# Two PSUM banks as one tile, or as two tiles and later one: an attention and gated feed-forward kernel

## The chip, the cores and the metric

The kernel runs on one core of one Trainium2 chip. The metric is device time in microseconds (us); lower is better. Three runs of the kernel before gave 505.23, 505.27 and 505.43 us, median 505.27.

The engines are called as in the profile: PE (TensorE, with its weight loads as PEld), DVE (VectorE), ACT (ScalarE), POOL (GpSimd), SP (SyncE, which here only issues DMAs). PSUM is the memory that PE writes its products to, in eight banks; DVE and ACT read it.

## What is computed

Attention in chunks of 64 positions, then a feed-forward block with a gate made by a convolution over the sequence. Sizes: batch 8, 8 heads, sequence 576, head size 64, so x is 8 x 576 x 512; w_in is 512 x 1024, w_out 1024 x 512.

```python
scores = scale * q_c @ k_c.T                    # per chunk of 64 positions
attn = softmax(scores);  out = attn @ v_c
x = out.transpose(0, 2, 1, 3).reshape(B, S, H * D)
h = relu(x @ w_in)
conv_out[t] = w[0] * h[t - 1] + w[1] * h[t] + w[2] * h[t + 1]
y = (h * sigmoid(conv_out)) @ w_out
```

## The kernel before

The 4608 rows of x are worked in 36 tiles of 128 rows (two chunks each) for the attention, and in 16 units of 288 columns for the feed-forward. A unit has eight blocks, one for each 128 of the 1024 inner features. Each product with the weights is three matmuls on rounded high and low parts (`x_h`, `x_l`, `wi_h`, `wi_l` and so on).

A **block** is a chain over one PSUM bank: `mm1` (PE, L330, twelve matmuls of 128x290), `h_relu` (ACT, L337, in place in the bank), `c_mid` (ACT, L342, reads the bank), `c_left` and `c_right` (DVE, L346 and L352, read the bank), `c_sig` (ACT, L358, works on `c` in SBUF), `c_mul` (DVE, L361, reads the bank for the last time), then `g_hi` (ACT, L371) and `g_lo` (POOL, L375). An **output tile** is 24 matmuls `mm2` (PE, L384, 128x512) into one bank and one copy out `o_copy` (ACT, L389), which SP stores (L392). An **attention tile** is: transposes of q and k (`t_pe`, PE, L164, into a bank, copied out by ACT at L168; from tile 9 on DVE transposes from SBUF at L173), `scores` (PE, L196), the softmax, a transpose of the probabilities (`p_pe`, PE, L265, into a bank, copied out by ACT at L270, up to tile 11; later tiles use a DMA and DVE), `attn_v` (PE, L279), and the copies into `x_h` and `x_l` (ACT L315, DVE L319).

**The eight banks.** Two always belong to the scores (the tile `sx`, named `sx_ps`). Six, numbered 0 to 5 by the plan, rotate among `mm1`, `mm2`, the q and k transposes and the probability transposes; a step takes a bank (`take=[("bk", ...)]`) and another frees it. After attention tile 11 two of the six go to the scores for good: the steps `give_up` take them and hand out two more score slots (`sx_half`, slots 0 and 1). Which two these are comes out of the plan (`lent["y", 0]`, `lent["y", 1]`); here they are 0 and 2. In the kernel before they are the two halves of one tile of 2 x 512 columns, `pair` (named `y_ps`), from the first instruction to the last. So y_ps in the rows means: up to about 140 us bank 0 or bank 2 of the six, later the third and fourth bank of the scores. The other four are tiles of one bank each (`b1_ps`, `b3_ps`, `b4_ps`, `b5_ps`, shown as b_ps).

**What orders the work.** All steps are listed with costs and needs, and a long list of numbers (`order_`) sets their order by hand. Each engine runs its instructions in that order; nothing overtakes. The plan counts banks as six separate things. The waits between engines are not written by hand: the tile layer below the kernel puts a wait on every instruction that touches a tile for what touched the same tile before it on another engine.

Two plan steps, `lend` and `give_up`, stand on POOL at no cost and issue nothing. Ahead of the steps the last loop (L898 to L904) also puts in transposes of the identity (L902) where the plan sees PE idle in the first 110 us.

Of the kernel before, what the change touches and what calls it, by code (L numbers as in the profile page):

```python
# [20 lines left out]
F32 = mybir.dt.float32  # L21
# [5 lines left out]
PSUM = bass.MemoryType.PSUM  # L27
# [3 lines left out]
def attn_ffn(ctx: ExitStack, tc: tile.TileContext, q, k, v, w_in, conv_w, w_out, out):  # L31
# [4 lines left out]
    P = 128  # L36
# [32 lines left out]
    ps_b = ctx.enter_context(tc.tile_pool(name="ps_b", bufs=1, space=PSUM))  # L69
# [11 lines left out]
        return s  # L81

    sx = ps_s.tile([P, 2, 512], F32, name="sx_ps")
    pair = ps_b.tile([P, 2, 512], F32, name="y_ps")
    banks = [None] * 6
    ident = const.tile([P, P], F32, name="ident")
    make_identity(nc, ident)
    rebias = const.tile([P, 1], F32, name="rebias")
# [86 lines left out]
    def sx_half(i):  # L175

        cols = slice(G * C * (i % 2), G * C * (i % 2) + G * C)
        return (sx if i // 2 else pair)[:, :, cols]

    def sx_bank(i, u):  # L180
        return sx_half(i)[:, u, :]
# [2 lines left out]
        pass  # L184

    def give_up(st):
        pass

    def scores(st):

# [12 lines left out]
    def s_max(st):  # L203
        st["m"] = work.tile([P, 2, G], F32, name="m")
        sv = sx_half(st["s"]).rearrange("p u (g j) -> p u g j", j=C)
        nc.vector.tensor_reduce(out=st["m"], in_=sv, op=ALU.max, axis=AX.X)

    def s_sub(st):
        st["e"] = work3.tile([P, H, C], F32, name="e")
        nc.vector.tensor_tensor(  # L210
            out=st["e"].rearrange("p (g u) j -> p u g j", u=2), in0=sx_half(st["s"]).rearrange("p u (g j) -> p u g j", j=C),
            in1=st["m"].rearrange("p u (g o) -> p u g o", o=1).broadcast_to([P, 2, G, C]), op=ALU.subtract)
# [312 lines left out]
    def att(t, key, load_key, writes):  # L525
# [36 lines left out]
        if t == PAIR - 1:  # L562
            a = step("POOL", 0.0, key, give_up, (lent,), [s], take=[("bk", lent, ("y", 0))])
            step("POOL", 0.0, key, give_up, (lent,), [a], take=[("bk", lent, ("y", 1))], free=[("sx", "l0"), ("sx", "l1")])
# [53 lines left out]
    group_loads, before, lent = {}, {"new": [], "x": []}, {}  # L618
# [62 lines left out]
    for u in range(NU + 1):  # L681
# [15 lines left out]
        for i, t in enumerate(outs_in[u] if u <= NU - 1 else []):  # L697
            st = {}
# [153 lines left out]
    for i in order_:  # L852
# [4 lines left out]
        for r in s["take"]:  # L857
            r, st, name = (r, None, None) if isinstance(r, str) else (r + r[:1])[:3]
            since, b = min(free_buf[r])
# [26 lines left out]
        for r in s["free"]:  # L886
            r, name = (r, r) if isinstance(r, str) else r
            b = s["args"][0][name] if r in ("slot", "wslot", "sx", "bk") else held[r][0]
# [2 lines left out]
            if r == "bk":  # L891
                taken[b][-1][1] = end[i]

    lent_ = [lent["y", 0], lent["y", 1]]
    for i in range(6):
        banks[i] = pair[:, lent_.index(i), :] if i in lent_ else ps_b.tile([P, 512], F32, name=f"b{i}_ps")
    pe_free, until_ = 2.0, 110.0
    for i in sorted(order_, key=lambda i: begin[i]):  # L898
        if steps[i]["eng"] == "PE" and begin[i] <= until_:
# [37 lines left out]
```

## Time and profile before

One profiled execution, as the profile's page has it:

| | |
|---|---|
| time of the profiled execution | 505.31 us |
| its span, first to last instruction | 503.3 us, so 2.0 us lie around it |
| median of three runs | 505.27 us |
| PE busy | 488.8 us, 97% of the span |
| DVE, ACT, POOL busy | 353.2, 299.4, 194.4 us |
| granted TensorE clock | full, in all 40 slices |
| chain of work that ended last | 85% PE, 5% DVE, 4% SP |

The waits view says for each engine what it stood idle for; the timeline has in brackets the idle time ahead of an instruction and the instruction that ended it. Both leave out the shortest pauses. The windows view has the busy time of each engine in a stretch.

### The profile page before, as it was taken

The page shows a single profiled execution, that of the slowest core. Times are in us where ns is not written, and L with a number is a line of the kernel's source. Part 1 is how long each engine was busy: PE and PEld are TensorE (multiplying, and loading weights), DVE is VectorE, ACT ScalarE, POOL GpSimd, SP SyncE. Part 2 cuts the span into 40 slices and gives each one's busy share as a digit, 9 for nine tenths or more (in the row PEclk, how much of TensorE's full clock was granted, in tenths as well). Part 3 has the DMA queues.
Part 4 walks back from the last instruction along what each step waited for, and adds up shares of the span by engine and source line. Part 5 has one row for each costly group of instructions (what it writes and reads, how often), then busy time and mean ns, then how long its engine had stood idle before and what let it go on. Part 6 is the DMA issues. An engine that isn't in the chain of part 4 may idle for free.

```text
span 503.3 us, 12909 instructions
## 1 busy us (share of the span) xinstructions
PE 488.8 (97%) x4985; PEld 435.8 (87%) x4985; DVE 353.2 (70%) x736; ACT 299.4 (59%) x749; POOL 194.4 (39%) x261
## 2 busy tenths in 40 slices
PE   8899899989999999999999999999999999999997
PEld 8788779877779898999988989899988998999885
DVE  3889789585757597987866798889778785574300
ACT  4477887765445375675653767667556565685501
POOL 1352457522351334446170445433353606144300
PEclk9999999999999999999999999999999999999999
DMA  8989945433236565424657362335463021000102
GB/s 204 227 225 248 215 132 87 76 50 58 42 91 121 111 140 114 93 56 91 128 105 177 74 124 51 85 69 109 100 146 96 23 63 44 30 35 1 42 22 83
DMA packets 185905, 50.16 MB, mean 100 GB/s; under 512 B 175068, under 2 KB 178164, under 8 KB 185844
## 3 DMA queue, kind: packets, MB, share of 16 engines
q1 hardware_dynamic: 185844, 49.34, 43.8%
q8 instruction: 39, 0.64, 0.6%
q14 instruction: 22, 0.18, 0.1%
HBM read 36.72 MB, written 9.44 MB: 92 GB/s over the span
## 4 chain that ended last, share of the span: by engine, by line
PE 85%; DVE 5%; SPq 4%; ACT 3%; issue 1%; DMA 1%; POOL 0%; ACTq 0%; DVEq 0%; POOLq 0%
PE b_ps L384 38%; PE b_ps L330 34%; SPq L139 4%; PE y_ps L330 3%; PE sx_ps L196 2%; PE sx_ps L279 2%; PE y_ps L279 1%; PE b_ps L902 1%; PE y_ps L196 1%; DMA qk<-in_moe_w_in 1%; DVE wt L426 1%; DVE c L352 1%; PE b_ps L265 1%; DVE wt L431 1%; PE y_ps L384 1%
## 5 line engine op out<-in xcount | busy, mean ns | idle before, releaser
L375 POOL TENSOR_TENSOR g_l<-c,g_h 128x288 fp32r<-128x288 f32 (+8 forms) x184 | 111.1, 626 | 161.9 <-ACT g_h L371 154.3
L384 PE MATMUL b_ps<-wo_h,g_h 128*128 128x512 f32 x280 | 112.4, 402 | 0.6 <-DVE c L361 0.6
L384 PE MATMUL b_ps<-wo_h,g_l 128*128 128x512 f32 x280 | 110.4, 394 | 0.0
L384 PE MATMUL b_ps<-wo_l,g_h 128*128 128x512 f32 x280 | 110.3, 394 | 0.0
L346 DVE SCALAR_TENSOR_TENSOR c<-b_ps,cw,c 128x287 f32<-128x287 f32 (+1 forms) x116 | 59.0, 511 | 43.7 <-ACT c L342 43.6
L358 ACT ACTIVATE c<-c 128x288 f32<-128x288 f32 x128 | 56.3, 442 | 45.0 <-DVE c L352 44.4
L330 PE MATMUL b_ps<-x_h,wi_h 128*128 128x290 f32 x464 | 82.1, 299 | 0.4 <-ACT y_ps L337 0.4
L330 PE MATMUL b_ps<-x_l,wi_h 128*128 128x290 f32 x464 | 81.2, 297 | 0.0
L330 PE MATMUL b_ps<-x_h,wi_l 128*128 128x290 f32 x464 | 80.7, 296 | 0.0
L330 PEld LDWEIGHTS b_ps<-x_h,wi_h 128*128 128x128 f32 x464 | 72.0, 189 | 8.4 <-DVE c L361 1.1
L337 ACT ACTIVATE b_ps<-b_ps 128x290 f32<-128x290 f32 x116 | 46.1, 399 | 50.2 <-PE b_ps L330 49.7
L361 DVE SCALAR_TENSOR_TENSOR c<-c,b_ps 128x288 f32<-128x288 f32 x116 | 51.5, 446 | 27.1 <-ACT c L358 26.1
L330 PEld LDWEIGHTS b_ps<-x_l,wi_h 128*128 128x128 f32 x464 | 68.7, 190 | 0.3 <-DVE x_l L319 0.3
L330 PEld LDWEIGHTS b_ps<-x_h,wi_l 128*128 128x128 f32 x464 | 68.3, 189 | 0.0
L371 ACT CAST g_h<-c 128x288 fp32r<-128x288 f32 (+8 forms) x184 | 58.6, 357 | 10.8 <-DVE c L361 8.8
L384 PEld LDWEIGHTS b_ps<-wo_h,g_l 128*128 128x128 f32 x280 | 52.7, 188 | 12.3
L384 PEld LDWEIGHTS b_ps<-wo_h,g_h 128*128 128x128 f32 x280 | 52.8, 189 | 10.1 <-DVE c L361 1.2
L342 ACT ACTIVATE c<-b_ps,cw 128x288 f32<-128x288 f32 x116 | 57.4, 499 | 6.9 <-POOL g_l L375 0.4
L352 DVE SCALAR_TENSOR_TENSOR c<-b_ps,cw,c 128x288 f32<-128x288 f32 (+1 forms) x116 | 58.8, 511 | 2.6
L384 PEld LDWEIGHTS b_ps<-wo_l,g_h 128*128 128x128 f32 x280 | 52.7, 188 | 8.1
L241 POOL TENSOR_TENSOR wt<-wt,z 128x512 f32<-128x512 f32 x24 | 25.0, 1050 | 68.4 <-DMA qk<-in_k 21.7
L389 ACT ACTIVATE wt<-b_ps 128x512 f32<-128x512 f32 x35 | 20.8, 598 | 35.8 <-PE b_ps L384 33.7
(89 smaller groups left out, 589.8 us busy)
## 6 DMA issues: line engine op xcount, KB each, us to landing
out<-wt SPq DMA_DIRECT2D x36, 256.0 KB, 2.3
v<-in_v SPq DMA_DIRECT2D x21, 256.0 KB, 3.7
qk<-in_q SPq DMA_DIRECT2D x96, 48.0 KB, 2.3
qk<-in_k SPq DMA_DIRECT2D x96, 48.0 KB, 2.2
qk<-in_moe_w_out SPq DMA_DIRECT2D x4, 1024.0 KB, 5.9
v<-in_v SPq DMA_DIRECT2D x48, 64.0 KB, 4.2
wt<-wt SPq DMA_DIRECT2D x48, 64.0 KB, 2.1
qk<-in_q SPq DMA_DIRECT2D x96, 24.0 KB, 1.9
```

Of the source, the lines that this page charges most:

```text
L241: nc.gpsimd.tensor_tensor(out=two(st, "to"), in0=two(st, "of"), in1=z, op=ALU.mult)
L330: nc.tensor.matmul(h_ps[:, 0:hi - lo], lhsT=wt[:, f // 2, kt, P * (f % 2):P * (f % 2) + P], rhs=xt[:, u % NX, kt, 0:hi - lo], start=n == 0 ...
L337: nc.scalar.activation(out=h, in_=h, func=AF.Relu)
L342: nc.scalar.mul(out=st["c"], in_=banks[st["h"]][:, i0:i0 + st["n"]], mul=cw[:, FT + f:FT + f + 1])
L346: nc.vector.scalar_tensor_tensor(out=c[:, a:n], in0=banks[st["h"]][:, i0 + a - 1:i0 + n - 1], scalar=cw[:, f:f + 1], in1=c[:, a:n], op0=AL ...
L352: nc.vector.scalar_tensor_tensor(out=c[:, 0:b], in0=banks[st["h"]][:, i0 + 1:i0 + 1 + b], scalar=cw[:, 2 * FT + f:2 * FT + f + 1], in1=c[: ...
L358: nc.scalar.activation(out=st["c"], in_=st["c"], func=AF.Tanh, scale=0.5)
L361: nc.vector.scalar_tensor_tensor(out=st["c"], in0=st["c"], scalar=1.0, in1=banks[st["h"]][:, st["i0"]:st["i0"] + st["n"]], op0=ALU.add, op ...
L371: nc.scalar.copy(out=g_h[:, f, gs], in_=st["c"][:, cs])
L375: nc.gpsimd.tensor_tensor(out=g_l[:, f, gs], in0=st["c"][:, cs], in1=g_h[:, f, gs].bitcast(F32), op=ALU.subtract)
L384: nc.tensor.matmul(banks[st["o"]], lhsT=gt[:, f, o:o + P], rhs=wt[:, f, :], start=f == 0 and n == 0, stop=f == FT - 1 and n == 2)
L389: nc.scalar.mul(out=st["os"], in_=banks[st["o"]], mul=0.5)
```

## The change

The two lent banks are no longer one tile. They come as two tiles of one bank each from a pool of their own, `ps_y`. When `give_up` runs for the second time, while the program is being built, that pool is closed, and a new pool `ps_z` is opened in its place, with one tile `z_ps` of 2 x 512 columns that holds both banks. `sx_half` takes that tile for slots 0 and 1. No instruction is added, taken away or put elsewhere on any engine; the tiles lie in other banks (sx 0 and 1 as before; the four b tiles in 2 to 5 instead of 4 to 7; the lent pair in 6 and 7 instead of 2 and 3).

```diff
     sx = ps_s.tile([P, 2, 512], F32, name="sx_ps")
-    pair = ps_b.tile([P, 2, 512], F32, name="y_ps")
     banks = [None] * 6
+    ps_y = ExitStack()
...
-        return (sx if i // 2 else pair)[:, :, cols]
+        return (sx if i // 2 else lent["pair"])[:, :, cols]
...
     def give_up(st):
-        pass
+
+        st["given"] = st.get("given", 0) + 1
+        if st["given"] == 2:
+            ps_y.close()
+            st["pair"] = ctx.enter_context(tc.tile_pool(name="ps_z", bufs=1, space=PSUM)).tile([P, 2, 512], F32, name="z_ps")
...
-    lent_ = [lent["y", 0], lent["y", 1]]
+    early_banks = ps_y.enter_context(tc.tile_pool(name="ps_y", bufs=1, space=PSUM))
     for i in range(6):
-        banks[i] = pair[:, lent_.index(i), :] if i in lent_ else ps_b.tile([P, 512], F32, name=f"b{i}_ps")
+        banks[i] = (early_banks if i in (lent["y", 0], lent["y", 1]) else ps_b).tile([P, 512], F32, name=f"b{i}_ps")
```

What the diff does not show is which waits stand on the instructions. The next rows are ACT's, around the first probability transpose that uses a lent bank; y_ps_86 is the pair, and each wait names the engine it is for.

```order
L270 COPY pT_799<-y_ps_86 128x512 [waits DVE_49,PE_49]
L315 CAST x_h_99<-sx_ps_85 128x4x128
L219 ACTIVATE e_754<-e_754 128x512
L371 CAST g_h_101<-c_656 128x288 [waits DVE_49]
L337 ACTIVATE y_ps_86<-y_ps_86 128x290 [waits PE_49,Activation_49]
L467 CAST wo_h_97<-wt_712 128x1024 [waits DVE_49]
L168 COPY qT_835<-y_ps_86 128x512 [waits Activation_49]
```

The same seven instructions of the changed kernel; b0_ps_108 and b2_ps_110 are the two lent banks.

```order
L274 COPY pT_803<-b2_ps_110 128x512 [waits PE_49]
L319 CAST x_h_98<-sx_ps_85 128x4x128 [waits DVE_49,PE_49]
L223 ACTIVATE e_758<-e_758 128x512
L375 CAST g_h_100<-c_660 128x288 [waits DVE_49]
L341 ACTIVATE b0_ps_108<-b0_ps_108 128x290 [waits PE_49]
L471 CAST wo_h_96<-wt_716 128x1024 [waits DVE_49]
L168 COPY qT_839<-b2_ps_110 128x512 [waits PE_49]
```

The instructions and their order are the same (lines are four further down). The copy of the probabilities, pT, reads bank 2; it no longer waits for DVE, and its wait for PE is for its own four transposes instead of for the `mm1` that PE puts into bank 0 after them. `h_relu` on bank 0 waits for its own `mm1` instead of for the q transposes that PE puts into bank 2 after it.

On PE the same is seen a little earlier. These six rows of before are the `mm1` into bank 1, then the transposes of the probabilities into bank 2 (y_ps_86), then `attn_v`.

```order
L330 MATMUL b1_ps_106<-x_h_99,wi_h_95 128x290 x4
L330 MATMUL b1_ps_106<-x_l_100,wi_h_95 128x290 x4
L330 MATMUL b1_ps_106<-x_h_99,wi_l_96 128x290 x4
L265 MATMUL y_ps_86<-ident_87,e_634 128x128 [waits DVE_49,Activation_49,Pool_49]
L265 MATMUL y_ps_86<-ident_87,e_634 128x128 x3
L279 MATMUL sx_ps_85<-pT_652,v_602 64x64 [waits DMAHW2_49,DVE_49]
```

And of the changed kernel:

```order
L334 MATMUL b1_ps_109<-x_h_98,wi_h_94 128x290 x4
L334 MATMUL b1_ps_109<-x_l_99,wi_h_94 128x290 x4
L334 MATMUL b1_ps_109<-x_h_98,wi_l_95 128x290 x4
L269 MATMUL b2_ps_110<-ident_86,e_638 128x128 [waits Pool_49]
L269 MATMUL b2_ps_110<-ident_86,e_638 128x128 x3
L283 MATMUL sx_ps_85<-pT_656,v_606 64x64 [waits DMAHW2_49,DVE_49]
```

The first transpose keeps its wait for POOL, which makes its input, and has lost the two for DVE and ACT, which were for `c_right` and `c_mid` on bank 0. Over the whole program 63 of 6166 instructions on the five engines wait for something else than before, all of them up to the handing over of the two banks; the first matmul into `z_ps` waits for DVE, ACT and a DMA, as the first into the scores' half of the pair did.

## The prediction

> **What bounds the kernel now.** I read the page first, then the windows view in four stretches, then who waits for whom inside the one that has idle time, then the timeline around the pauses.
>
> ```profile
> span 503.3 us, 12909 instructions
> ...
> PE 488.8 (97%) x4985; PEld 435.8 (87%) x4985; DVE 353.2 (70%) x736; ACT 299.4 (59%) x749; POOL 194.4 (39%) x261
> ```
>
> ```profile
> 0.00:39.00 39.00, 35.28 (x488) 32.49 (x489) 26.39 (x52) 21.75 (x38) 13.38 (x16) 1.00 0.89 224
> 39.00:132.00 93.00, 85.96 (x888) 76.27 (x887) 72.75 (x146) 67.81 (x163) 41.79 (x45) 1.00 0.54 115
> 132.00:450.00 318.00, 317.99 (x3364) 285.05 (x3364) 241.44 (x514) 190.38 (x495) 125.99 (x175) 1.00 0.42 91
> 450.00:503.30 53.30, 49.61 (x250) 42.01 (x248) 12.66 (x26) 19.43 (x55) 13.27 (x26) 1.00 0.09 35
> ```
>
> The columns are the stretch, its length, busy time of PE, PEld, DVE, ACT and POOL, then clock and DMA. PE sets the time: 97% of the span, and from 132 to 450 us 317.99 of 318.00. So time gained on PE before 132 comes off the end one for one, if nothing else holds it up later. The first 39 us hold filler transposes and first loads, and the last 53 the tail; the change has nothing there to remove but a small part. What is to be had lies in 39 to 132: 93.00 - 85.96 = 7.04 us of idle PE. PE's waits there, in total us, times, longest:
>
> ```profile
> PE y_ps L330 <- DVE c L361: 1.4, 2, 0.7
> PE y_ps L330 <- ACT y_ps L337: 1.1, 1, 1.1
> PE y_ps L330 <- ACT c L342: 0.9, 1, 0.9
> PE y_ps L330 <- DVE c L352: 0.8, 1, 0.8
> PE y_ps L265 <- DVE c L361: 0.7, 1, 0.7
> PE y_ps L164 <- ACT pT L270: 0.7, 1, 0.7
> PE b_ps L384 <- DVE c L361: 0.6, 1, 0.6
> PE y_ps L384 <- ACT c L342: 0.4, 1, 0.4
> PE b_ps L330 <- ACT y_ps L337: 0.4, 1, 0.4
> ```
>
> Ten pauses, 7.0 us, and they account for all of the idle time. Eight stand before a matmul that writes y_ps, though y_ps is two of six banks. And the releasers are odd. A matmul may begin a bank anew when `c_mul` (L361) has read it for the last time; here PE goes on after `h_relu` (L337), `c_mid` (L342) or `c_right` (L352), with `c_mul` of that block still to come. So the bank that PE writes is not the bank that was being read: it is the other half of the pair.
>
> **What the pairing costs, seen at one place.** Timeline rows: start, length, what, and in brackets the idle time before it and who ended it. The first two show an undisturbed `mm1` for comparison.
>
> ```profile
> 40.02 0.69 PE L330 MATMUL y_ps<-x_h,wi_h 128*128 128x290 f32 x4
> 40.56 0.70 PE L330 MATMUL y_ps<-x_l,wi_h 128*128 128x290 f32 x4
> ...
> 49.82 0.59 ACT L270 COPY pT<-y_ps 128x512 f32<-128x512 f32 x1 [1.71 <-PE y_ps L330]
> 50.46 0.66 PE L164 MATMUL y_ps<-ident,qk 128*128 128x128 f32 x4 [0.68 <-ACT pT L270]
> ...
> 53.72 0.51 ACT L342 ACTIVATE c<-y_ps,cw 128x288 f32<-128x288 f32 x1
> 54.28 0.81 PE L330 MATMUL y_ps<-x_h,wi_h 128*128 128x290 f32 x4 [0.92 <-ACT c L342]
> 54.92 0.71 PE L330 MATMUL y_ps<-x_l,wi_h 128*128 128x290 f32 x4
> ```
>
> At 49.82 ACT copies transposed probabilities out of bank 2. What it copies is written by L265, yet it stood idle 1.71 us for an L330, the `mm1` into bank 0. Having been held, it holds PE at 50.46, whose transposes need bank 2. At 54.28 PE begins an `mm1` in bank 2 and has waited for `c_mid` on bank 0.
>
> Each stop costs more than its idle time. Undisturbed, four matmuls last 0.69 us but the next four begin 0.54 after them (40.02 to 40.56): 0.15 overlap, lost when PE drains. After the stop the step from the first four to the next is 0.64 (54.28 to 54.92), 0.10 more. So a stop costs its idle time and about 0.25 us.
>
> ACT and DVE pay too. Of their waits in the same stretch, those released by a matmul that makes nothing they read:
>
> ```profile
> ACT c L342 <- PE y_ps L330: 2.4, 2, 1.5
> ACT pT L270 <- PE y_ps L330: 1.7, 1, 1.7
> ACT pT L270 <- PE y_ps L384: 1.6, 1, 1.6
> DVE c L346 <- PE y_ps L330: 3.7, 2, 2.0
> DVE c L361 <- PE y_ps L330: 2.1, 1, 2.1
> DVE c L361 <- PE y_ps L384: 1.0, 1, 1.0
> ```
>
> 5.7 us on ACT and 6.8 on DVE. `c_mid` and `c_left` come after `h_relu` of their own bank, so by then their `mm1` is long done.
>
> **The change, part by part.** *Two tiles in place of one, up to the handing over.* It takes off waits, and adds and moves no instruction, DMA or queue. Five of the eight y_ps pauses lose the wait that ended them, since that reader is on the other bank: the two released by L342, those released by L352 and L337, and, by the waits of the built programs, one of the two L330 released by L361. The other three have a true last wait that came late: the copy at 49.82 for 50.46, and twice a `c_mul` that DVE reached late (for the other L330, and for L265). The two pauses before b_ps are of the same kind, one bank further off:
>
> ```profile
> 105.64 0.50 ACT L342 ACTIVATE c<-y_ps,cw 128x288 f32<-128x288 f32 x1 [0.95 <-PE y_ps L330]
> 105.87 0.50 PE L384 MATMUL b_ps<-wo_h,g_h 128*128 128x512 f32 x1 [0.64 <-DVE c L361]
> 107.19 0.76 PE L330 MATMUL b_ps<-x_h,wi_h 128*128 128x290 f32 x4 [0.37 <-ACT y_ps L337]
> ```
>
> At 105.64 `c_mid` waits 0.95 us for a foreign `mm1`, and ACT and DVE, each in its order, bring everything behind it late, the `c_mul` of banks 1 and 3 among it. So I take all ten: 7.0 us idle + 10 x 0.25 = 9.5 us.
>
> What is late next? DVE has 72.75 us of work for the stretch; in 93.0 - 9.5 = 83.5 us that is 87%, with 10.8 us of room, and 6.8 us of what it now idles goes away as well. ACT has 67.81, or 81%. Loads: none of these waits of PE names a DMA. I charge nothing for a new wait, and keep it as a rival.
>
> *The new pool and its tile.* The first scores in `z_ps` must wait for the last readers of both lent banks. The latest is a `c_mul`; PE, behind which everything would stand, comes there much later (a row of the timeline, and one of the chain of waits: start, length, what):
>
> ```profile
> 139.76 0.40 DVE L361 SCALAR_TENSOR_TENSOR c<-c,y_ps 128x288 f32<-128x288 f32 x1
> ```
>
> ```profile
> 150.87 0.62 PE y_ps L279 x32
> ```
>
> 150.87 - 140.16 = 10.7 us of room. PE and that `c_mul` move forward together, so it costs nothing; were PE's whole gain not shared by DVE, 1.2 us would still be left. Nor does the choice of bank numbers: no row ties a length to one.
>
> *After the handing over* PE needs its loads earlier by as much as it comes earlier. SP's queue, its waits in 130 to 172 us and its rows on either side of the longest:
>
> ```profile
> SPq L392 <- ACT wt L389: 10.4, 1, 10.4
> ```
>
> ```profile
> 130.66 2.58 SPq L156 DMA_DIRECT2D v<-in_v  x4
> 143.71 2.05 SPq L392 DMA_DIRECT2D out<-wt  x2
> ```
>
> SP stands 10.4 us at 143.71 behind the store of an output tile, which waits for `o_copy`, so for PE. With PE 9.5 us ahead, the store and the loads queued behind it come 9.5 us ahead, just inside SP's own 133.24. So the loads move along.
>
> **Sum.** The profiled execution took 505.31 us (span 503.3, 2.0 around it), as good as the median of 505.27. 505.3 - 9.5 = **495.8 us**. If the rest of this holds, 494.3 to 497.3: less 1.5 if three stops keep half their price; and 1.5 better, since the view leaves out short stops, and the twelve `mm1` blocks in the pair could each hide 0.12 us.
>
> **Rivals.** A difference of 0.2% (1.0 us) is about what a measurement of this kernel can tell from none.
>
> *Real shortage of banks.* The pauses would mean that six banks are too few, and new true waits would take the place of the old. For it: the two pauses before b_ps. Against: from 140 us on the same two products have four banks, and PE is never idle up to 450. If half of the stops stay, the gain is 4.7 us: 500.6. The Trainium skill (Perfetto Trace Analysis, Optimization Strategy) says that a gap that keeps repeating on the engine that should be saturated can mean too little PSUM for the next tile; read so, all ten stops would stay, and the time with them. The trace speaks for that only as far as the two b_ps rows go. Chance 0.13.
>
> *The gain is given back after 132 us.* SP has only 0.9 us between its own end (133.24) and the new time of that store (134.2). If issue or landing of the loads, and not PE, sets the pace from there, PE runs dry by up to 9.5 us before 175 and the kernel ends at 505.3. Against: SP's 10.4 us wait. Chance 0.04.
>
> *The change doesn't do what it says*, the layer below still tying the two tiles together: 505.3. The rows of waits speak against it. Chance 0.02.
>
> *Slower: DVE becomes the bound.* More of DVE's work would fall beside POOL's (41.79 us here), and if they slow each other, DVE's 72.75 us grow. PE comes out behind once DVE needs over 93 us, a stretch of 28%; at 35% it needs 98.2 and the time is about 510.5. Against: POOL is busy in 45% of this stretch already (41.79 of 93), and `c_right` on the pair has this spread (shortest, median, longest ns):
>
> ```profile
> L352 DVE SCALAR_TENSOR_TENSOR c<-y_ps,cw,c x12: 474/516/518, 45.7 to 138.3; 128x288 f32<-128x288 f32 x6, 128x287 f32<-128x287 f32 x6
> ```
>
> No instruction there is stretched. Chance 0.02.
>
> **How the numbers follow.** The forecast has 0.79, the shortage 0.13, the gain given back 0.04, no effect of the edit 0.02, slower 0.02. The range takes the forecast's bounds and reaches into the shortage, to where a little under half of the stops stay: 494.3 to 499.5. Faster 0.79 + 0.13 = 0.92, same 0.04 + 0.02 = 0.06, slower 0.02.
>
> **What would show it.** Right: idle PE in the stretch that now is 39 to 132 falls from 7.04 us to under 1, no PE wait between 39 and 123 us named for a reader of another bank, no ACT L270 released by an `mm1`, the first `attn_v` in the new tile at about 141.4 instead of 150.87, SP's longest wait before its store still there but short, and PE without idle from there to the tail. Wrong: PE pauses of the same number before the lent banks (shortage, or no effect), or PE idle between 130 and 175 behind SP or a DMA (given back), or DVE instructions longer than in the rows above (slower).

## The result and the profile after

The changed kernel took 497.84 us (median of 4 runs, 497.11 to 498.99), before 505.35 on the same chip: ratio 0.985, 95% interval 0.9827 to 0.9873. The forecast was 495.8 us, in a range of 494.3 to 499.5. The profiled execution took 497.11 us. In the code after, lines are four further down (`mm1` is L334, `attn_v` L283, `p_pe` L269, `c_mul` L365, `w_sgn` L435, POOL's subtraction `w_left` L439, ACT's cast `w_hi` L471).

The head of the page and its engines, after:

```profile
span 495.1 us, 12901 instructions
...
PE 484.8 (98%) x4985; PEld 435.6 (88%) x4985; DVE 353.1 (71%) x736; ACT 298.6 (60%) x749; POOL 194.5 (39%) x261
```

PE's busy time fell by 4.0 us with the same 4985 matmuls: a stop costs more than its idle time, and the rest counts as busy (of the 10.0 us that the ten places returned, see below, 7.0 were idle). The stretches, in the windows view (length, then PE, PEld, DVE, ACT, POOL, clock, DMA):

```profile
0.00:39.00 39.00, 32.45 (x472) 29.46 (x473) 26.47 (x49) 20.17 (x36) 12.31 (x16) 1.00 0.87 210
39.00:123.00 84.00, 84.00 (x898) 77.96 (x897) 73.42 (x150) 68.19 (x164) 41.84 (x44) 1.00 0.59 130
123.00:132.00 9.00, 9.00 (x73) 7.30 (x72) 6.18 (x14) 4.59 (x11) 1.05 (x3) 1.00 0.35 64
132.00:441.00 309.00, 309.00 (x3297) 278.24 (x3296) 233.65 (x499) 185.40 (x484) 125.91 (x174) 1.00 0.43 93
```

All ten pauses are gone: from 39 us to the tail PE is never idle. But the first stretch got worse: 32.45 us busy in 39 where before had 35.28. PE's longest wait of the whole program, after:

```profile
PE sx_ps L283 <- ACT wi_h L471: 2.2, 1, 2.2
...
```

This line is new; the view has four more, all in the first 39 us, and all of them were there before. (One of them, at 11.24 us, grew from 0.17 to 0.92 us, but only because PE came to it 0.75 us sooner.) Pairing every matmul with the same matmul of before gives the whole account, in the times of the changed kernel: it is 2.08 us late after 32.72 us, level with before at 54.4, 7.94 us ahead at 120, and 8.2 ahead from 300 us to the end. So the ten places, with shorter ones between them, returned 10.0 us, later places 0.3, and one new place took 2.1: 505.31 - 8.2 = 497.1.

The new place, in the timeline of before (start, length, engine, line):

```profile
26.96 0.59 ACT L168 COPY qT<-y_ps 128x512 f32<-128x512 f32 x1 [0.55 <-PE y_ps L265]
27.92 1.06 ACT L467 CAST wi_h<-wt 128x1024 fp32r<-128x1024 f32 x1
28.52 0.69 DVE L431 SCALAR_TENSOR_TENSOR wt<-qk,wt 128x512 uint32<-128x512 uint32 x1
29.06 3.63 POOL L435 TENSOR_TENSOR wi_l<-wt,wi_h 128x1024 fp32r<-128x1024 f32 x2 [1.58 <-ACT wi_h L467]
30.64 0.69 PE L279 MATMUL sx_ps<-pT,v 64*64 64x64 f32 x32
```

and after:

```profile
26.30 0.57 ACT L168 COPY qT<-b_ps 128x512 f32<-128x512 f32 x1
27.25 1.06 ACT L471 CAST wi_h<-wt 128x1024 fp32r<-128x1024 f32 x1
28.38 2.37 POOL L439 TENSOR_TENSOR wi_l<-wt,wi_h 128x1024 fp32r<-128x1024 f32 x1 [0.91 <-ACT wi_h L471]
28.51 2.78 DVE L435 SCALAR_TENSOR_TENSOR wt<-qk,wt 128x512 uint32<-128x512 uint32 x1
31.93 0.69 DVE L214 TENSOR_TENSOR e<-sx_ps,m 128x512 f32<-128x512 f32 x1
32.72 0.69 PE L283 MATMUL sx_ps<-pT,v 64*64 64x64 f32 x32 [2.24 <-ACT wi_h L471]
```

Read them from the top. ACT's copy of qT lost a false wait for the transposes of `p_pe` in the other lent bank, and starts 0.66 us sooner. Its cast wi_h does too, so POOL's subtraction starts at 28.38 instead of 29.06. DVE's `w_sgn` stands where it stood, at 28.5, but POOL is now 0.13 us ahead of it, and `w_sgn` takes 2.78 us instead of 0.69, until just after POOL's end at 30.75. The `attn_v` at 32.72 overwrites what DVE's L214 reads, so it waits for that (31.93 + 0.69 = 32.62); the view names ACT's wi_h, which had ended at 31.95.

### The profile page after: what moved, and what is told of

The parts are those of the page before. It is cut to its first block, busy times and chain, and to the rows that moved or that the text cites. A ratio compares the mean times of both kernels' runs of the same rounds, so it can differ in the third digit from the quotient of the medians.

```text
span 495.1 us, 12901 instructions
## 1 busy us (share of the span) xinstructions
PE 484.8 (98%) x4985; PEld 435.6 (88%) x4985; DVE 353.1 (71%) x736; ACT 298.6 (60%) x749; POOL 194.5 (39%) x261
## 4 chain that ended last, share of the span: by engine, by line
PE 93%; DVE 4%; DMA 1%; ACT 1%; issue 1%; ACTq 0%; DVEq 0%
PE b_ps L334 42%; PE b_ps L388 41%; PE sx_ps L283 3%; PE sx_ps L200 3%; PE z_ps L283 1%; DVE wt L435 1%; PE b_ps L164 1%; PE z_ps L200 1%; PE b_ps L906 1%; DMA qk<-in_moe_w_in 1%; PE b_ps L269 1%; DVE wt L430 1%; DVE wt L425 0%; DVE z L230 0%; DVE e L214 0%
## 5 line engine op out<-in xcount | busy, mean ns | idle before, releaser
L350 DVE SCALAR_TENSOR_TENSOR c<-b_ps,cw,c 128x287 f32<-128x287 f32 (+1 forms) x128 | 65.1, 510 | 46.0 <-ACT c L346 45.8
L334 PE MATMUL b_ps<-x_h,wi_h 128*128 128x290 f32 x512 | 90.7, 299 | 0.0
L334 PE MATMUL b_ps<-x_l,wi_h 128*128 128x290 f32 x512 | 89.5, 297 | 0.0
L334 PE MATMUL b_ps<-x_h,wi_l 128*128 128x290 f32 x512 | 89.1, 296 | 0.0
L334 PEld LDWEIGHTS b_ps<-x_h,wi_h 128*128 128x128 f32 x512 | 79.3, 189 | 7.8 <-DVE c L365 0.6
L365 DVE SCALAR_TENSOR_TENSOR c<-c,b_ps 128x288 f32<-128x288 f32 x128 | 56.6, 445 | 29.0 <-ACT c L362 28.0
L334 PEld LDWEIGHTS b_ps<-x_l,wi_h 128*128 128x128 f32 x512 | 75.9, 190 | 0.0
L334 PEld LDWEIGHTS b_ps<-x_h,wi_l 128*128 128x128 f32 x512 | 75.4, 189 | 0.0
L346 ACT ACTIVATE c<-b_ps,cw 128x288 f32<-128x288 f32 x128 | 63.2, 499 | 7.3 <-POOL g_l L379 0.4
L356 DVE SCALAR_TENSOR_TENSOR c<-b_ps,cw,c 128x288 f32<-128x288 f32 (+1 forms) x128 | 64.8, 510 | 2.8
L388 PEld LDWEIGHTS b_ps<-wo_h,g_h 128*128 128x128 f32 x288 | 54.4, 189 | 9.2
```

Source lines behind the costliest of these rows:

```text
L334: nc.tensor.matmul(h_ps[:, 0:hi - lo], lhsT=wt[:, f // 2, kt, P * (f % 2):P * (f % 2) + P], rhs=xt[:, u % NX, kt, 0:hi - lo], start=n == 0 ...
L346: nc.scalar.mul(out=st["c"], in_=banks[st["h"]][:, i0:i0 + st["n"]], mul=cw[:, FT + f:FT + f + 1])
L350: nc.vector.scalar_tensor_tensor(out=c[:, a:n], in0=banks[st["h"]][:, i0 + a - 1:i0 + n - 1], scalar=cw[:, f:f + 1], in1=c[:, a:n], op0=AL ...
L356: nc.vector.scalar_tensor_tensor(out=c[:, 0:b], in0=banks[st["h"]][:, i0 + 1:i0 + 1 + b], scalar=cw[:, 2 * FT + f:2 * FT + f + 1], in1=c[: ...
L365: nc.vector.scalar_tensor_tensor(out=st["c"], in0=st["c"], scalar=1.0, in1=banks[st["h"]][:, st["i0"]:st["i0"] + st["n"]], op0=ALU.add, op ...
L388: nc.tensor.matmul(banks[st["o"]], lhsT=gt[:, f, o:o + P], rhs=wt[:, f, :], start=f == 0 and n == 0, stop=f == FT - 1 and n == 2)
```

## The experiments

Three theories of what was seen. **Collision** (the texts written before the runs call it the port theory): `w_sgn` reads two tiles of SBUF, POOL's subtraction reads SBUF, and whichever starts first holds up the other; the loss is 2.1 us, and the order of the two is all that matters. **Load**: `w_sgn` was long because its data came late or by chance. **Banks**: part of the gain or loss comes from the new pool and the new bank numbers. All kernels but one are the changed kernel with a list of added waits: ("ACT", 19, "PE", 220) makes ACT's instruction number 19, counted from 0, wait for PE's number 220.

**The changed kernel once more**, on the chip of the next three, as a control.

> The changed kernel, unaltered, once more, as the ground for the other three. Two theories. Port theory: one DVE instruction at about 28.5 us (the last step of preparing a weight block, 0.69 us before, 2.78 us in the profile of the changed kernel) is held by a POOL instruction that starts 0.1 us ahead of it, because an ACT copy lost a wait and the chain from ACT to POOL came 0.67 us earlier; this is in the program, so it is there in every execution: again 2.7 to 2.8 us, time 497 to 499. Load theory: the 2.1 us slip between 28 and 36 us comes of when the loads landed in that execution; then the DVE instruction is 0.7 us in some executions, and the time of this run may be 495.5.

498.06 us (497.18 to 498.82), ratio 0.9845 [0.9824, 0.9867]. Its profiled execution took 498.48 us, with these waits of PE among others:

```profile
PE sx_ps L283 <- ACT wi_h L471: 2.4, 1, 2.4
...
PE b_ps L334 <- issue: 0.8, 1, 0.8
...
PE b_ps L164 <- DMA qk<-in_k: 0.4, 1, 0.4
```

The new wait is there again. The two small ones and 0.2 us on the first are the 1.4 us by which this span (496.5) is longer than the first one's. The long `w_sgn` in both executions speaks against the load theory.

**ACT's false wait back.** The qT copy alone waits again for the `p_pe` in the other bank.

```diff
+    waits = [("ACT", 19, "PE", 220)]
```

> The changed kernel with one of the lost waits put back: ACT's copy of the transposed q at about 26.3 us waits again for the probability transposes in the other lent bank. Nothing else differs. Port theory: the copy is back at 26.96 us, POOL's instruction back at about 29.06, behind the start of the DVE instruction, which takes 0.69 us again; 2.1 us come off the changed kernel, to about 495.7 us, although a wait was added. Load theory: the loads are as they were, the time is that of the changed kernel, 497 to 499.

494.88 us (494.68 to 495.21), ratio 0.9786 [0.9772, 0.9801]: 3.2 us under the changed kernel on the same chip, and no run of the one reaches a run of the other. The collision accounts for 2.1 of the 3.2 (the spans of the profiled executions are 495.1 and 492.9 us). The other 1 us is that the runs of the changed kernel spread from 497.1 to 499.0, and these only from 494.7 to 495.2; why, no run shows. Its timeline at the place:

```profile
26.98 0.58 ACT L168 COPY qT<-b_ps 128x512 f32<-128x512 f32 x1 [0.55 <-PE b_ps L269]
...
28.54 0.69 DVE L435 SCALAR_TENSOR_TENSOR wt<-qk,wt 128x512 uint32<-128x512 uint32 x1
...
29.08 3.63 POOL L439 TENSOR_TENSOR wi_l<-wt,wi_h 128x1024 fp32r<-128x1024 f32 x2 [1.58 <-ACT wi_h L471]
...
30.66 0.70 PE L283 MATMUL sx_ps<-pT,v 64*64 64x64 f32 x32
```

A wait that is good for nothing in itself makes the kernel faster: DVE is first again, `w_sgn` takes 0.69 us, and PE starts at 30.66 without a pause that the view shows.

**POOL waits instead.** All false waits stay away; POOL's subtraction waits for `w_sgn`.

```diff
+    waits = [("POOL", 9, "DVE", 35)]
```

> The changed kernel with one new wait: POOL's instruction at 28.4 us (low part of a weight block, 128x1024) waits until the DVE instruction that it held up is done. ACT's copy stays early. Port theory: POOL starts at about 29.3 instead of 28.4, DVE takes 0.69 us, and 2.1 us come off: 495.7 us, as with the wait put back by the other means. Load theory: no change, 497 to 499.

495.62 us (495.22 to 496.17), ratio 0.9801 [0.9786, 0.9816].

```profile
28.63 0.69 DVE L435 SCALAR_TENSOR_TENSOR wt<-qk,wt 128x512 uint32<-128x512 uint32 x1
...
29.47 3.60 POOL L439 TENSOR_TENSOR wi_l<-wt,wi_h 128x1024 fp32r<-128x1024 f32 x2 [1.88 <-ACT pT L274]
30.76 0.69 PE L283 MATMUL sx_ps<-pT,v 64*64 64x64 f32 x32 [0.16 <-issue]
```

ACT is early here and DVE is still not held, so it is POOL's start that decides, not ACT's. Both came out within 1 us of the 495.7 that the collision theory gave. The load theory falls.

**The pair one tile, the new pool kept.** The two lent banks are one tile until they are given up; pool, handing over and bank numbers are those of the changed kernel, and the waits on the instructions are those of before.

```diff
+    lent_ = [lent["y", 0], lent["y", 1]]
+    pair = early_banks.tile([P, 2, 512], F32, name="y_ps")
     for i in range(6):
-        banks[i] = (early_banks if i in (...) else ps_b).tile([P, 512], F32, name=f"b{i}_ps")
+        banks[i] = pair[:, lent_.index(i), :] if i in lent_ else ps_b.tile([P, 512], F32, name=f"b{i}_ps")
```

> One part undone: the two lent banks are one tile again until they are given up, but in a pool of its own that is closed then, with the new tile in its place as in the changed kernel, and at the changed kernel's bank numbers. Coupling theory (the single tile tied two unrelated banks together, and PE's ten pauses came of it): all of the gain is gone, 505.3 us, with PE's pauses of 7.0 us back. Rival (the new pool or the other bank numbers bring the gain): 497 to 499, or something between.

505.63 us (504.94 to 506.7), ratio 0.9999 [0.9989, 1.001]. Every pause of before is back at its place and length; three of the ten in its timeline of PE:

```profile
112.77 0.78 PE L334 MATMUL y_ps<-x_h,wi_h 128*128 128x290 f32 x4 [0.65 <-DVE c L365]
123.16 0.77 PE L334 MATMUL y_ps<-x_h,wi_h 128*128 128x290 f32 x4 [0.80 <-DVE c L356]
126.80 0.80 PE L334 MATMUL y_ps<-x_h,wi_h 128*128 128x290 f32 x4 [1.11 <-ACT y_ps L341]
```

So pool and bank numbers bring nothing; the tying of the two banks is the whole effect, of both signs.

**Whose waits were they?** The kernel with ACT's wait back (494.88) is the changed one without the collision, and before is that kernel with all other false waits. The next two put back one half each: PE's twelve, or the other 39, on ACT and DVE; with ACT's wait, these are all that the tied pair adds. They and the last two kernels ran on another chip, on which before took 505.3 us instead of 505.5; differences to 494.88 are good to a few tenths of a us.

```diff
+    waits = [("ACT", 19, "PE", 220), ("PE", 428, "DVE", 62), ("PE", 428, "ACT", 45), ...]
```

> The kernel with ACT's wait (494.88 us), and the twelve waits that PE's instructions had through the pairing put back as well; ACT's and DVE's stay away. Bounds: 494.88 us without any of them, 505.5 with all. Step of the prediction: five pauses, 3.9 us idle in all, were ended by a foreign reader on PE itself, and five more, 3.1 us, came from ACT and DVE being late. If both halves add up, with 0.25 us a stop, this kernel costs 3.9 + 5 x 0.25 = 5.1 us: 500.0. Rival 1, PE's own waits are the whole: 505. Rival 2, they bite only because ACT and DVE are late, and alone cost little: under 496.5.

496.45 us (496.29 to 496.48), ratio 0.9824 [0.981, 0.9837]: 1.6 us, not 5.1. All of PE's pauses between 39 and 132 us:

```profile
52.88 0.79 PE L334 MATMUL b_ps<-x_h,wi_h 128*128 128x290 f32 x4 [0.36 <-ACT c L346]
85.44 0.50 PE L388 MATMUL b_ps<-wo_h,g_h 128*128 128x512 f32 x1 [0.17 <-ACT c L346]
```

The counterpart:

```diff
+    waits = [("ACT", 19, "PE", 220), ("ACT", 43, "PE", 387), ("ACT", 44, "ACT", 43), ..., ("DVE", 60, "PE", 387), ...]
```

> The counterpart: the kernel with ACT's wait (494.88 us), and the other waits of ACT and DVE for work in the foreign bank put back; PE's stay away. If the halves add up: 3.1 us idle in five pauses, with 5 x 0.25 us, 4.4 us: 499.3. Rival 1 (PE's own waits are the whole): 495. Rival 2 (lateness of ACT and DVE is the whole): 505. If this kernel and its counterpart together cost clearly more or less than the 10.6 us between 494.88 and 505.5, the waits of the engines feed each other.

501.08 us (500.61 to 501.31), ratio 0.9915 [0.9901, 0.9928]: 6.2 us. Its pauses in the same stretch:

```profile
50.70 0.66 PE L164 MATMUL b_ps<-ident,qk 128*128 128x128 f32 x4 [0.68 <-ACT pT L274]
53.79 0.81 PE L334 MATMUL b_ps<-x_h,wi_h 128*128 128x290 f32 x4 [0.20 <-ACT qT L168]
59.97 0.80 PE L334 MATMUL b_ps<-x_h,wi_h 128*128 128x290 f32 x4 [0.72 <-DVE c L365]
69.38 0.63 PE L269 MATMUL b_ps<-ident,e 128*128 128x128 f32 x4 [0.72 <-DVE c L365]
104.65 0.50 PE L388 MATMUL b_ps<-wo_h,g_h 128*128 128x512 f32 x1 [0.64 <-DVE c L365]
105.97 0.78 PE L334 MATMUL b_ps<-x_h,wi_h 128*128 128x290 f32 x4 [0.36 <-ACT b_ps L341]
```

The halves cost 1.6 and 6.2 us, together 7.8 of the 10.6 us between this base and before; the other 2.8 us need both. With PE's waits alone PE hardly ever stops, since ACT and DVE are then early enough. Held themselves by a foreign matmul, they come late to the reads for which PE waits: the pauses at 112.77, 123.16 and 126.80 above stand in neither half.

**Can the collision of before be had too?** Before already has one at 20 us, in its timeline:

```profile
18.72 1.04 POOL L258 TENSOR_TENSOR e<-e,z 128x512 f32<-128x512 f32 x1 [7.15 <-DVE z L232]
19.05 1.79 DVE L426 SCALAR_TENSOR_TENSOR wt<-qk,wt 128x1024 uint32<-128x1024 uint32 x1
19.73 2.26 POOL L435 TENSOR_TENSOR wi_l<-wt,wi_h 128x512 fp32r<-128x512 f32 x1
20.88 2.18 DVE L431 SCALAR_TENSOR_TENSOR wt<-qk,wt 128x1024 uint32<-128x1024 uint32 x1
```

The two DVE instructions, with two SBUF inputs each, take 1.79 and 2.18 us (1.22 elsewhere) beside POOL's work. The next two kernels hold that POOL instruction too until DVE is through, one with ACT's wait, one with POOL's.

```diff
+    waits = [("ACT", 19, "PE", 220), ("POOL", 6, "DVE", 23)]
```

> The kernel with ACT's wait (494.88 us), and POOL's wi_l of 128x512 at 19.75 us held until DVE has done both instructions with two SBUF inputs that it stretches (1.79 and 2.18 us instead of 1.22 each at full length). If POOL's reading of SBUF stretches them, DVE comes 1.0 to 1.5 us sooner to the softmax at 23.01, PE's pause of 1.2 us before attn_v at 24.52 falls to some 0.2 us, and the time is 493.8 us (0.2% less). If that pause has another cause (ACT or a load), 494.9; if the later wi_l holds PE up at its first mm1, over 495.5.

495.22 us (494.47 to 495.48), ratio 0.9798 [0.9784, 0.9811].

```diff
+    waits = [("POOL", 6, "DVE", 23), ("POOL", 9, "DVE", 35)]
```

> The same without ACT's wait: both of POOL's wi_l instructions, that at 19.75 and that at 28.4 us, are held until DVE is through with the instructions with two SBUF inputs beside them. If both collisions are POOL's reading of SBUF: 495.6 (only the second held) less 1.0, 494.6 us; if the first costs PE nothing, 495.6; if one of the two is due to something else, its DVE instruction stays long, and the time is 495.6 to 498.

494.86 us (494.76 to 495.23), ratio 0.9794 [0.9781, 0.9808]. Neither can be told from 494.88. DVE in this second one:

```profile
19.08 1.79 DVE L430 SCALAR_TENSOR_TENSOR wt<-qk,wt 128x1024 uint32<-128x1024 uint32 x1
20.90 1.23 DVE L435 SCALAR_TENSOR_TENSOR wt<-qk,wt 128x1024 uint32<-128x1024 uint32 x1
...
22.65 0.86 DVE L233 TENSOR_SCALAR z<-z 128x8 f32<-128x8 f32 x1
23.43 0.68 DVE L214 TENSOR_TENSOR e<-sx_ps,m 128x512 f32<-128x512 f32 x1
```

and POOL beside it, with the PE instruction that waits for L214:

```profile
18.75 1.04 POOL L262 TENSOR_TENSOR e<-e,z 128x512 f32<-128x512 f32 x1 [7.15 <-DVE z L236]
22.21 1.27 POOL L439 TENSOR_TENSOR wi_l<-wt,wi_h 128x512 fp32r<-128x512 f32 x1 [2.42 <-DVE wt L435]
```

```profile
24.20 0.69 PE L283 MATMUL sx_ps<-pT,v 64*64 64x64 f32 x32 [0.92 <-issue]
```

L435 is freed (1.23 us instead of 2.18), and POOL's subtraction takes 1.27 us instead of 2.26. L430 stays at 1.79: it was held by POOL's L262, not by the subtraction. And POOL, moved to 22.21, now stands in the way of the small L233 (0.86 us where 0.16 is usual). PE comes 0.3 us sooner, not 1.0. In the first of the two that 0.3 us is lost again at a pause of 0.57 us behind a late ACT:

```profile
44.67 0.69 PE L200 MATMUL sx_ps<-kT,qT 64*64 64x64 f32 x32 [0.57 <-ACT kT L168]
```

The lateness began with a load. In that execution ACT waited 1.53 us for a block of weights, on which it starts at 36.54 us in the kernel of 494.88, and DVE and ACT's next `wi_h` passed the delay on:

```profile
37.85 1.13 ACT L421 ACTIVATE wt<-qk 128x1024 f32<-128x1024 f32 x1 [1.53 <-DMA qk<-in_moe_w_in]
```

In the second kernel ACT starts on it at 36.62. SP issued its loads of w_in later in the first (the second of two at 30.78 instead of 29.30 us in the kernel of 494.88); why, isn't settled.

## Why the prediction was right, and where it was off

**Idle PE between 39 and 132 us is the cost of the tying.** Right, and shown: with the tying the pauses are there (505.63 us), without it none, and the ten places return 10.0 us. The shortage of banks falls, and with it the reading of repeated gaps after the Trainium skill (Perfetto Trace Analysis, Optimization Strategy): all ten gaps left with no PSUM added.

**A stop costs its idle time and 0.25 us.** Right. Between the kernel with ACT's wait and the tied pair PE loses 9.30 us at the ten stops, whose idle time in the view is 6.97 us: 0.23 us each. Places too short for the view cost 0.65 more, and 0.6 us comes at 177 and 296 us; together 10.6, which is the difference of the spans to 0.1 us (503.4 - 492.9). The prediction had these short stops in its range, not in its sum. What the 0.6 us late in the kernel are isn't settled.

**Five pauses from PE's own waits, five from ACT and DVE.** Half right. The second five come back whole with the waits of ACT and DVE alone (0.68, 0.72, 0.72, 0.64 and 0.36 us, as in before). Of the first five, PE's waits alone bring back 0.36 and 0.17 us. The prediction priced each wait by itself; the waits feed each other.

**"I charge nothing for a new wait."** This step failed, and it cost 2.1 us. It rested on two others. "The change has nothing there to remove but a small part", of the first 39 us, was true of what it removes; but one of the lost waits lies there, on ACT's qT copy, and its going moved POOL ahead of DVE. And "No instruction there is stretched" was read from `c_right`, which has only one input in SBUF; the other is a bank. Where DVE reads two tiles of SBUF, before already showed 2.18 us for 1.22 at 20.88. And within the stretch itself, 39 to 132 us, the timeline of before has a POOL and a DVE instruction that were stretched (1.04 and 1.22 us elsewhere):

```profile
74.23 1.82 POOL L258 TENSOR_TENSOR e<-e,z 128x512 f32<-128x512 f32 x1 [4.17 <-DVE z L232]
```

```profile
76.89 1.46 DVE L426 SCALAR_TENSOR_TENSOR wt<-qk,wt 128x1024 uint32<-128x1024 uint32 x1
```

So the mechanism of the slower rival is real, but as a meeting of two instructions, not as a load on DVE: 2.1 us once, not 35% of a stretch.

The sum again with both: 505.3 - 10.6 + 2.1 = 496.8; the profiled execution took 497.11, the median of all is 0.7 above that.

The time is in the range partly by luck. The forecast's own bounds were 494.3 to 497.3, and the median of 497.84 lies above them. The range reached on to 499.5 for another reason, a shortage of banks that would keep some of the stops, and no stop stayed. The gain from the ten places was right (9.5 us forecast, 10.0 measured); what filled the upper part of the range was the new wait, priced at nothing, and the spread of the runs.

**The handing over and SP's queue.** Right. The first matmul in the new tile, and SP's longest wait at that time, after:

```profile
142.86 0.69 PE L283 MATMUL z_ps<-pT,v 64*64 64x64 f32 x32
```

```profile
SPq L396 <- ACT wt L393: 4.9, 1, 4.9
```

In the timeline of before this matmul starts at 150.80 (150.87 was from the chain of waits). So it comes 7.9 us sooner, not the 9.5 that gave 141.4: 10.0 us returned, less 2.1. PE did not wait for it, SP's wait shrank from 10.4 to 4.9 us and did not vanish (more was left than the 0.9 us forecast, since SP's own work ended at 130.80 instead of 133.24), and PE has no idle time behind it. The gain was not given back, and the rival by which the edit would do nothing falls with the pauses.

## What to carry to other kernels

To the dependency tracking seen here a tile of two banks is one thing: two unrelated uses of its halves wait for each other on PE, ACT and DVE, and such waits show as a releaser that works on another bank than the waiting instruction. When waits go, list not only who was waiting but which pairs of DVE and POOL instructions change their order, in every stretch where a changed wait stands: there a gain of 0.7 us on ACT cost 2.1 us on PE. Waits on several engines can't be priced one by one; here the parts sum to 7.8 us and the whole to 10.6.

## What the hardware showed

Two kinds of DVE instructions and POOL's excluded each other for whole instructions: those with two inputs in SBUF, and tensor_scalar. The one that started second was held until the first had ended. `w_sgn` at 28.51 ended 0.54 us after POOL's end (0.69 alone). POOL's L262 in the timeline of after, and DVE's L425 beside it:

```profile
26.43 1.04 POOL L262 TENSOR_TENSOR e<-e,z 128x512 f32<-128x512 f32 x1 [0.75 <-ACT wt L421]
...
26.75 1.00 DVE L425 TENSOR_SCALAR wt<-wt 128x512 uint32<-128x512 uint32 x1
```

L425 ended 0.28 us after POOL (0.43 alone), and L233 above 0.03 us after it (0.16 alone): each time what it needs alone less 0.13 to 0.15 us. So the price can be estimated beforehand from these rows: what is left of the first instruction at the start of the second, less some 0.14 us. The Trainium skill (SBUF — State Buffer, Who interferes with whom) says that a DVE instruction with two SBUF inputs contends with a GpSimd instruction that reads SBUF, that tensor_scalar can as well in its two-port modes, that tensor_reduce doesn't, and that the order of issue decides who is blocked. The traces agree: L425 and L233 are tensor_scalar with one input (whether they ran in such a mode the traces don't say); the reduce L230 took 0.69 us beside POOL's L262 as elsewhere; and `c_right`, with one input in a bank, stays within 460 to 520 ns in all 128 instructions, though POOL was at work beside 73 of them (shortest, median, longest):

```profile
L356 DVE SCALAR_TENSOR_TENSOR c<-b_ps,cw,c x128: 460/516/520, 44.9 to 466.3; 128x288 f32<-128x288 f32 x64, 128x287 f32<-128x287 f32 x64
```

A look at `c_right` alone could not have shown the collision.
